# Delta-rule attention and a top-2 router in one kernel: gathered rows regrouped by transfers and turned by VectorE

## The chip, the cores and the metric

The kernel runs on one core of a Trainium2 chip. The metric is the time of one execution on the device in microseconds; lower is better. The core has five instruction queues that matter here. TensorE (PE) multiplies matrices, and its weight loads have a row of their own, PEld. VectorE (DVE), ScalarE (ACT) and GpSimd (POOL) do the elementwise work. SyncE (SP) issues transfers; GpSimd issues the indirect ones, which gather or scatter rows by a list of row numbers. Each queue runs in order, and the queues meet at semaphores.

## The reference

```python
batch, n_heads, seq, head_dim = (4, 8, 768, 48)
for t in range(S):                        # delta rule, one state per (batch, head)
    kt, vt, bt = (k_n[:, :, t], v[:, :, t], beta[:, :, t, None])
    y[:, :, t] = np.einsum('bhd,bhde->bhe', q[:, :, t], state)
    v_old = np.einsum('bhde,bhd->bhe', state, kt)
    state = state + bt[:, :, :, None] * np.einsum('bhd,bhe->bhde', kt, vt - v_old)
...
x = np.ascontiguousarray(attn_out.transpose(0, 2, 1, 3)).reshape(B * S, H * D)   # 3072 x 384
noisy_logits = x @ w_gate + np.log1p(np.exp(x @ w_noise)) * noise                # 8 experts
top2 = np.argpartition(-noisy_logits, 2, axis=1)[:, :2]
...
for e in range(E):
    for k in range(2):
        mask = top2[:, k] == e
        h = np.maximum(x[mask] @ w1[e], 0.0)          # 384 -> 1024
        out[mask] += top2_w[mask, k, None] * (h @ w2[e])   # 1024 -> 384
```

Each of 3072 tokens goes through two of eight experts. All arithmetic is in float32.

## The kernel before

**Two stages.** `deltanet` computes the recurrence in chunks of 64 tokens and, as tokens become ready, routes them. A small planner (`Jobs`) gives every piece of work an engine, a cost and a due time, and writes out the order of all engines, SP and GpSimd among them. Then the experts run one after another in an order that the code itself gives, for PE, ACT, DVE and GpSimd; SP is left to the scheduler there.

**The table of tokens.** Router results go to a table in HBM, `tokens_x`, with three floats a row: the token's number, its gate, and the row of `rows_y` where its 384 attention outputs lie. `spread` (L431) scatters them, `load_metas` (L417) and early loads (L1268) read them back as lists. Numbers are stored as floats, so `numbers` (L427, L428, and L1277, L1278 for the early tiles) has VectorE convert them to integers before an indirect transfer can use them. `take_rows` (L396) gathers rows of `rows_y` by such a list, 128 tokens to a tile; `add_rows` (L450) adds finished rows to the output.

**Expert 0** is done mostly inside the first stage. As soon as the first tiles of its tokens are known, `early` gathers them, turns them on PE (L1302), and multiplies (L1321, L1345). Five tiles are done so. What is left, one tile and 64 rows, is `rest` (L1688 to L1720): it uses `rest_x`, whose gathers stand at the end of the first stage. This place, between the stages, is called the seam. `rest` also prepares expert 1: it gathers its rows (`load_rows`), forms the sums of its first weights (`SUMS_W`, on VectorE here), turns its rows and forms the sums of them (`SUMS_X`).

**Experts 1 to 7** have six tiles of 128 tokens and one of 64 each, 832 columns. Both products use schemes with fewer multiplications on sums of blocks: `first` (the hidden layer, L1576 into `inner`, twenty block products) and `second` (L1576 into `outer` and `inner`, seven products for each of three pairs of tiles, added to `sums` by VectorE at L1475 and L1479). `both(n)` is step n for the first two pairs. While expert e runs, the rows of e + 1 are gathered into one of two buffers `xr` after `first`; `turn_rows` (L1591, L1596) turns a tile by three TensorE transpositions into a PSUM bank and a copy by ScalarE, two tiles after each of four `both` calls; then come `SUMS_X` (L1542) on VectorE and `SUMS_W` on GpSimd. A bank of PSUM can only be reused when the add that reads it is done.

Of the kernel before, what the change touches and what calls it, by code (L numbers as in the profile page):

```python
# [9 lines left out]
FP32 = mybir.dt.float32  # L10
I32 = mybir.dt.int32
# [10 lines left out]
Q = 32  # L22
TILES = 6
MORE = 64
EARLY_BANK = 2, (0, 1, 2)
EARLY = {1: [(0, 2)], 3: [(2, 4)], 4: [(4, 5)]}
EARLY_TILES = 5
ROWS = TILES * 128 + MORE
# [53 lines left out]
BANKS_C, TURN_BANKS, LAST_BANK = (1, 2, 4), (3, 0), 4  # L82
# [149 lines left out]
def kernel(  # L232
# [110 lines left out]
    w1r = moe_w1.rearrange("e (do di) f -> e di do f", di=128)  # L343
    w2r = moe_w2.rearrange("e (fo fi) d -> e fi fo d", fi=128)

    def weight_tiles(pool):
        return (
            pool.tile([128, KT, F], FP32, name="w1e"),
            pool.tile([128, FT, DM], FP32, name="w2e"),
        )  # L350

# [42 lines left out]
    def take_rows(got, index, units):  # L394
# [13 lines left out]
    indices, places = (  # L408
        const.tile([128, E, TILES + 1], I32, name=x) for x in ("indices", "places")
    )  # L410
# [15 lines left out]
    def numbers(e, t):  # L426
        nc.vector.tensor_copy(places[:, e, t], metas_x[:, e, t, 2])  # L427
        nc.vector.tensor_copy(indices[:, e, t], metas_x[:, e, t, 0])  # L428
# [31 lines left out]
    def deltanet(ictx):  # L460
# [593 lines left out]
        def route(g):  # L1054
# [91 lines left out]
            def counted():  # L1146
# [12 lines left out]
                        metas(g)[:, 0:units, :, x],  # L1159
# [54 lines left out]
        def cut(s, rows):  # L1214
# [21 lines left out]
        early_index, early_place = (  # L1236
            sb([128, EARLY_TILES], x, I32) for x in ("early_index", "early_place")
        )
        early_meta = sb([128, EARLY_TILES, META], "early_meta")

        def put_early(got, at):
            d = add_rows(got, early_index[:, at : at + 1], "out0", added)
            early_out.append(d)
            return d

        early_x = [sb([128, DM], f"early_x{i}") for i in range(4)]
# [9 lines left out]
        def early(s, lo, hi):  # L1256
# [19 lines left out]
            def numbers():  # L1276
                nc.vector.tensor_copy(early_place[:, lo:hi], early_meta[:, lo:hi, 2])  # L1277
                nc.vector.tensor_copy(early_index[:, lo:hi], early_meta[:, lo:hi, 0])  # L1278

# [3 lines left out]
            )  # L1283
            jobs.add(
                DVE, 0.4, numbers, reads=[("early_meta", lo)], writes=[("early_index", lo)],
                late=lo,
            )
            units = (s + 1) * US
            for i in range(n):
                at = lo + i  # L1290
                x, x_key = early_x[at % 4], ("early_x", at % 4)
                jobs.add(
                    POOL, 1.2,
                    lambda x=x, at=at: [take_rows(x, early_place[:, at : at + 1], units)],
                    reads=[("early_index", lo), *(("stored", i) for i in range(units))],
                    writes=[x_key], lands=2.0, moves=0.7, late=lo,
                )
                p = early_bank()

                def turned_rows(x=x, p=p):  # L1300
                    for do in range(KT):
                        nc.tensor.transpose(  # L1302
                            flat(p)[:, do * 128 : (do + 1) * 128],
                            x[:, do * 128 : (do + 1) * 128], ident,
                        )

                jobs.add(PE, 0.5, turned_rows, reads=[x_key], opens=p, late=lo)
                jobs.add(
                    ACT, 0.5,
                    lambda i=i, p=p: nc.scalar.copy(  # L1310
                        early_xe[:, :, i * 128 : (i + 1) * 128],
                        flat(p)[:, 0 : KT * 128].rearrange("p (k t) -> p k t", t=128),
                    ),
                    writes=[("early_xe", i)], closes=p, late=lo,
                )
# [21 lines left out]
            for i in range(n):  # L1337
# [3 lines left out]
                for f0 in range(0, FT, 2):  # L1341
# [19 lines left out]
                )  # L1361
                jobs.add(
                    POOL, 1.3,
                    lambda got=got, at=at: [put_early(got, at)],
                    reads=[got_key, ("early_index", lo), *(("cleared", i) for i in range(4))],
# [8 lines left out]
        held = {}  # L1374
# [14 lines left out]
        nc.gpsimd.memset(blanks[:, :, 0], float(N))  # L1389
# [48 lines left out]
        every = [("rows", x, i, y) for x in range(NS) for i in range(US) for y in (0, 1)]  # L1438
        for e in range(E):
            jobs.add(  # L1440
                SP, 0.7, lambda e=e: load_metas(e), reads=every, writes=[("metas", e)],
                lands=2.0, moves=0.3, late=EARLY_TILES - 0.5,
            )
        last_tiles = slice(EARLY_TILES, TILES + 1)
        jobs.add(
            DVE, 0.4, lambda: numbers(0, last_tiles), reads=[("metas", 0)],
            writes=["places"], late=EARLY_TILES - 0.5,
        )
        for i, size in enumerate(rows_in[last_tiles]):
            jobs.add(  # L1450
                POOL, 1.2,
                lambda i=i, size=size: take_rows(
                    rest_x[0:size, i],
                    places[0:size, 0, EARLY_TILES + i : EARLY_TILES + i + 1], NT,
                ),
                reads=["places", *(("stored", n) for n in range(NT))], writes=[("rest_x", i)],
                lands=2.0, moves=0.7, late=EARLY_TILES - 0.5,
            )
        jobs.add(
            DVE, 0.4, lambda: numbers(slice(1, E), slice(0, TILES + 1)),  # L1460
            reads=[("metas", e) for e in range(1, E)], writes=["all places"],
            late=EARLY_TILES - 0.4,
        )
# [4 lines left out]
        return held["w"]  # L1468

    with ExitStack() as ictx:  # L1470
        weights = deltanet(ictx)
# [15 lines left out]
    with ExitStack() as ectx:  # L1487
        ectx.enter_context(
            tc.manual_schedule(engines={*IN_ORDER, mybir.EngineType.Pool})
# [20 lines left out]
        xrs = [moe.tile([128, TILES + 1, DM], FP32, name=f"xr{i}") for i in range(2)]  # L1510
# [70 lines left out]
        def load_rows(e, tiles=range(TILES + 1)):  # L1581
            for i in tiles:
                take_rows(
                    xrs[e % 2][0 : rows_in[i], i], places[0 : rows_in[i], e, i : i + 1], NT
                )

        def turn_rows(e, i, banks=TURN_BANKS):
            xr, rows = xrs[e % 2], rows_in[i]
            p_xt = inner[banks[i % len(banks)]][:, 0 : KT * 128].rearrange("p (k t) -> p k t", t=128)
            for do in range(KT):  # L1590
                nc.tensor.transpose(  # L1591
                    p_xt[:, do, 0:rows], xr[0:rows, i, do * 128 : (do + 1) * 128],
                    ident[0:rows, 0:rows],
                )
            at = MAIN if rows < 128 else i * 128 + (MORE if i * 128 >= MAIN else 0)
            nc.scalar.copy(xe[:, :, at : at + rows], p_xt[:, :, 0:rows])  # L1596
# [78 lines left out]
        def rest():  # L1675
# [5 lines left out]
            got, gate = sums[0], metas_x[:, 0, :, 1]  # L1681
            load_rows(1)
            add_up(nc.vector, SUMS_W, blocks[0])
            xe_r = moe.tile([128, KT, cols], FP32, name="xe_r")
            for i, size in enumerate(rows_in[t0:]):
                p_xt = bank_x[i][:, 0 : KT * 128].rearrange("p (k t) -> p k t", t=128)
                for do in range(KT):
                    nc.tensor.transpose(  # L1688
                        p_xt[:, do, 0:size], rest_x[0:size, i, do * 128 : (do + 1) * 128],
                        ident[0:size, 0:size],  # L1690
                    )
                nc.scalar.copy(
                    xe_r[:, :, i * 128 : i * 128 + size], p_xt[:, :, 0:size]
                )
# [9 lines left out]
            for i in range(TILES + 1):  # L1704
                turn_rows(1, i, range(5))
# [7 lines left out]
            for fo in range(FT):  # L1713
# [9 lines left out]
                add_rows(got[0:size, i], indices[0:size, 0, t0 + i : t0 + i + 1], "out0", added)  # L1723
# [6 lines left out]
        index, gate = indices[:, 1], metas_x[:, 1, :, 1]  # L1730
        sums_of_second(blocks[1])
        for e in range(1, E):
# [6 lines left out]
            def put(i):  # L1739
                added.append(  # L1740
                    add_rows(
                        got[0 : rows_in[i], i], index[0 : rows_in[i], i : i + 1], f"out{e}",
                        earlier,
                    )
                )
# [23 lines left out]
            if follows:  # L1769
                load_rows(e + 1)  # L1770
                add_up(nc.gpsimd, SUMS_W, blocks[0])
# [8 lines left out]
            turns = iter(range(TILES + 1 if follows else 0))  # L1780
            sums_x = SUMS_X if follows else []
            for n in (5, 6, 3, 7, 4):
                both(n)
                for i in (next(turns, None), next(turns, None)):
                    if i is not None:
                        turn_rows(e + 1, i)
# [14 lines left out]
            if follows:  # L1801
                sums_of_second(blocks[1])
                index, gate = indices[:, e + 1], metas_x[:, e + 1, :, 1]
# [7 lines left out]
    with tc.If(count > ROWS):  # L1811
        for e in range(E):
            with tc.tile_pool(name=f"left{e}", bufs=1) as pool:
                w1e, w2e = load_weights(weight_tiles(pool), e)
                earlier, added = added, []
                for i in range(TILES, NT):
# [3 lines left out]
                    index, row = (pool.tile([128, 1], I32, name=x) for x in ("indexl", "rowl"))  # L1820
                    nc.vector.tensor_copy(index, meta[:, 0:1])
                    if i == TILES:
                        nc.vector.memset(index[0:MORE], N)
                    nc.vector.tensor_copy(row, meta[:, 2:3])
                    gate = meta[:, 1:2]
                    xr = pool.tile([128, DM], FP32, name="xrl")
                    take_rows(xr, row, NT)
# [3 lines left out]
                    for do in range(KT):  # L1831
                        nc.tensor.transpose(
                            p_xt[:, do], xr[:, do * 128 : (do + 1) * 128], ident
# [49 lines left out]
```

## Time and profile before

| | us |
|---|---|
| median of 3 runs (835.3 to 838.07) | 837.69 |
| the profiled execution | 832.74 |
| its span, from first to last instruction | 830.6 |
| `first` of expert 1 starts | 394.9 |
| one expert, from `first` to `first` | 60.6 |
| end of expert 7 on PE, about | 819 |

Times in a timeline are us from the start of the span. A row of it gives start, duration, engine, line, operation, output<-inputs, shapes, number of instructions merged, and in brackets how long the engine sat idle before and what released it. A row of the table by stage gives the stretch, its length, the busy time of PE, PEld, DVE, ACT and POOL, the granted TensorE clock as a share, the share of the DMA engines and GB/s. In the page, a digit is a fortieth of the span in tenths of busy time.

### The profile page before, as it was taken

Reading aid. Unit: us, or ns where it says so; the run is one execution under the profiler, and the core shown is the slowest. Engines: PE = TensorE matmul, PEld = TensorE weight load, DVE = VectorE, ACT = ScalarE, POOL = GpSimd, SP = SyncE. Lnnn points to the kernel's source line nnn. Section 1 sums busy time; section 2 is a strip of 40 time slices with the busy share of each in tenths; the row PEclk is TensorE's granted clock in tenths of the full one; section 3 lists DMA queues with packets and bytes.
Section 4 is the critical chain, followed back from the end, with each engine's and each line's share of the span. In section 5 each row is a group of like instructions: output and inputs, shape, how many; then the busy total and the mean of one; then the engine's idle time right before and its main releaser. Section 6 shows DMA issues by size and latency. Waiting matters only on the chain.

```text
span 830.6 us, 22834 instructions
## 1 busy us (share of the span) xinstructions
PE 734.5 (88%) x9512; PEld 577.3 (70%) x9512; DVE 550.6 (66%) x1238; ACT 332.1 (40%) x789; POOL 398.6 (48%) x377
## 2 busy tenths in 40 slices
PE   4656888786978889997999999999999999999993
PEld 3445777675767787774588588587597597597593
DVE  5899999998899343034676665665766765865841
ACT  3546585836582641122530531531521521511500
POOL 2102100134311815632885885885885786777022
PEclk9975868879798689998999999999999999999997
DMA  2465646533232311553523524425325235213022
GB/s 48 76 112 126 188 137 157 143 63 67 47 71 55 52 43 21 97 145 119 143 81 47 149 77 77 119 78 105 90 84 119 69 95 114 62 20 42 1 38 26
DMA packets 119888, 70.67 MB, mean 85 GB/s; under 512 B 93536, under 2 KB 114144, under 8 KB 119776
## 3 DMA queue, kind: packets, MB, share of 16 engines
q1 hardware_dynamic: 105056, 48.98, 22.4%
q0 software_dynamic: 12544, 19.75, 13.3%
q8 instruction: 77, 1.26, 0.7%
q10 hardware_dynamic: 2176, 0.39, 0.3%
q14 instruction: 35, 0.29, 0.1%
HBM read 49.85 MB, written 20.03 MB: 84 GB/s over the span
## 4 chain that ended last, share of the span: by engine, by line
PE 62%; DVE 20%; issue 10%; POOL 3%; DMA 2%; ACT 1%; SPq 1%; DVEq 0%; POOLq 0%; ACTq 0%
PE inner L1576 25%; PE outer L1576 14%; DVE part L737 6%; DVE t L741 5%; PE pair L1321 3%; PE pair L1345 3%; PE pair L606 2%; POOL out_dram L450 2%; PE inner L1591 2%; PE inner L1668 2%; PE single L588 2%; PE pair L924 1%; DVE t L656 1%; PE pair L983 1%; DVE qk L858 1%
## 5 line engine op out<-in xcount | busy, mean ns | idle before, releaser
L1618 DVE TENSOR_TENSOR hT<-hT,inner 128x416 f32<-128x416 f32 x182 | 105.4, 586 | 64.3 <-PE inner L1576 56.4
L450 POOL DMA_INDIRECT out_dram<-sums,indices x51 | 83.0, 1627 | 117.1 <-DVE sums L1479 68.8
L1624 ACT ACTIVATE hT<-inner 128x416 f32<-128x416 f32 x112 | 57.9, 517 | 173.0 <-PE inner L1576 172.2
L431 POOL DMA_INDIRECT tokens_x<-meta,slot x48 | 48.5, 1010 | 89.3 <-DVE r_d L1071 39.4
L1576 PE MATMUL inner<-s_x,w1e 128*128 128x416 f32 x196 | 78.7, 512 | 0.0
L737 DVE TENSOR_TENSOR part<-t 128x30 f32<-128x30 f32 (+9 forms) x180 | 70.7, 393 | 4.8
L741 DVE TENSOR_TENSOR t<-t,part 128x30 f32<-128x30 f32 (+9 forms) x180 | 63.0, 350 | 6.2
L1613 ACT ACTIVATE hT<-hT 128x416 f32<-128x416 f32 x112 | 59.8, 547 | 12.2 <-DVE hT L1618 7.2
L396 POOL DMA_INDIRECT xr<-rows_y,places x49 | 57.0, 1164 | 14.0 <-issue 13.1
L1576 PE MATMUL outer<-t_w,hT 128*128 128x192 f32 x336 | 59.7, 328 | 0.0
L1576 PEld LDWEIGHTS inner<-s_x,w1e 128*128 128x128 f32 x196 | 37.2, 190 | 31.2 <-issue 29.0
L706 POOL TENSOR_SCALAR_AFFINE_SELECT t<-t 128x1024 f32<-128x1024 f32 x6 | 7.6, 1267 | 106.5 <-DVE ss L677 106.5
L1576 PE MATMUL inner<-xe,w1e 128*128 128x416 f32 x140 | 58.1, 513 | 0.0
L1576 PE MATMUL inner<-s_x,s_w 128*128 128x416 f32 x140 | 56.9, 512 | 0.0
L1596 ACT COPY xe<-inner 128x384 f32<-128x384 f32 (+1 forms) x49 | 20.3, 459 | 90.8 <-PE inner L1591 90.8
L1576 PEld LDWEIGHTS outer<-t_w,hT 128*128 128x128 f32 x336 | 54.7, 190 | 0.4
L1576 PE MATMUL outer<-w2e,hT 128*128 128x192 f32 x280 | 50.1, 326 | 0.0
L1576 PEld LDWEIGHTS outer<-w2e,hT 128*128 128x128 f32 x280 | 46.5, 190 | 2.2 <-issue 2.2
L1542 POOL TENSOR_TENSOR w1e<-w1e 128x256 f32<-128x256 f32 x54 | 47.0, 878 | 2.0
L1475 DVE TENSOR_SCALAR sums<-outer,metas_x 128x192 f32<-128x192 f32 x70 | 28.0, 414 | 29.9 <-PE outer L1576 29.9
L888 POOL TENSOR_TENSOR v<-v,norms 128x384 f32<-128x384 f32 x24 | 22.7, 961 | 52.3 <-PE pair L606 41.9
L1576 PEld LDWEIGHTS inner<-s_x,s_w 128*128 128x128 f32 x140 | 26.6, 190 | 22.3 <-issue 22.3
(202 smaller groups left out, 1620.7 us busy)
## 6 DMA issues: line engine op xcount, KB each, us to landing
w1e<-in_moe_w_dram SPq DMA_DIRECT2D x8, 1536.0 KB
w2e<-in_moe_w_dram SPq DMA_DIRECT2D x8, 1536.0 KB
qp<-in_q_dram SPq DMA_DIRECT2D x48, 96.0 KB
v<-in_v_dram SPq DMA_DIRECT2D x48, 96.0 KB
out_dram<-empty SPq DMA_DIRECT2D x4, 1152.0 KB
rows_y<-y SPq DMA_DIRECT2D x24, 192.0 KB
kp<-in_k_dram SPq DMA_DIRECT2D x88, 48.0 KB
out_dram<-sums,indices POOLq DMA_INDIRECT x51, 4.4
```

What stands on the lines that cost most here:

```text
L396: d = nc.gpsimd.indirect_dma_start(out=got, out_offset=None, in_=rows_y[0 : units * 128], in_offset=bass.IndirectOffsetOnAxis(ap=index, ax ...
L431: d = nc.gpsimd.indirect_dma_start(out=tokens_x, out_offset=bass.IndirectOffsetOnAxis(ap=slot, axis=0), in_=meta, in_offset=None, bounds_c ...
L450: d = nc.gpsimd.indirect_dma_start(out=out, out_offset=bass.IndirectOffsetOnAxis(ap=index, axis=0), in_=got, in_offset=None, bounds_check= ...
L737: v_.tensor_tensor(out=part, in0=t[:, :, j + 1 :, j, None].to_broadcast(shape), in1=t[:, :, None, j, 0:j].to_broadcast(shape), op=ALU.mult,)
L741: columns[:] = [v_.tensor_tensor(out=t[:, :, j + 1 :, 0:j], in0=t[:, :, j + 1 :, 0:j], in1=part, op=ALU.add).ins]
L1321: nc.tensor.matmul(flat(p)[:, 0:rows], w1e[:, do, fo * 128 : (fo + 1) * 128], early_xe[:, do, 0:rows], start=(do == 0), stop=(do == KT - 1),)
L1475: nc.vector.tensor_scalar_mul(got, p, gate)
L1542: engine.tensor_tensor(out=block(to), in0=block(x), in1=block(y), op=ALU.add if sign == "+" else ALU.subtract,)
L1576: nc.tensor.matmul(p, lhsT, rhs, start=opens and i == 0, stop=i == len(products) - 1, skip_group_check=True,)
L1613: nc.scalar.activation(h, h, ACTF.Relu)
L1618: nc.vector.tensor_tensor(out=h, in0=h, in1=p, op=ALU.add if sign > 0 else ALU.subtract)
L1624: nc.scalar.mul(h, p, float(sign))
```

## The change

Five things are changed.

1. For experts 1 to 7 the gathered rows are no longer turned on TensorE. Sixteen transfers (`regroup`) move 32-row by 96-column pieces within SBUF from `xr` to a new tile `xq`, so that partition group c holds columns c*96 to c*96+95 of all tokens. Seven block transpositions of VectorE (`turns`), which turn 32x32 blocks in place of their partition group, then write `xe`. One buffer `xr` is left in place of two.
2. So that this gives a usable order, feature number di*3+do lies in partition di, chunk do (before: do*128+di). The first weights are loaded by that rule (`(di do)`), which makes 12 KB of each partition contiguous, and the blocks that TensorE still turns (early tiles, `rest_x`) are read with a step of three (`chunk`).
3. The table's numbers are integers kept in the bits of the float table; `numbers` and its tiles go.
4. At the seam, the lists, the gathers of `rest_x` and of expert 1's rows and `regroup` come first in GpSimd's order; three of the five additions of the early tiles (`held["puts"]`) come after them and after `SUMS_W`, which GpSimd does there now.
5. SP keeps the program's order in the second stage too: weights of expert 1, then the lists, `regroup`, weights of expert 2, and for each later expert its weights, then `regroup`.

```diff
-    w1r = moe_w1.rearrange("e (do di) f -> e di do f", di=128)
+    w1r = moe_w1.rearrange("e (di do) f -> e di do f", di=128)
+    def chunk(x, k):
+        return x[:, k:DM:KT]
...
-    def numbers(e, t):
-        nc.vector.tensor_copy(places[:, e, t], metas_x[:, e, t, 2])
-        nc.vector.tensor_copy(indices[:, e, t], metas_x[:, e, t, 0])
+    def number_of(meta):
+        return meta[..., 0:1].bitcast(I32)
+
+    def place_of(meta):
+        return meta[..., 2:3].bitcast(I32)
...
+                if s > PUT_IN_RULE:
+                    held["puts"].append(lambda got=got, at=at: put_early(got, at))
+                    continue
...
-        xrs = [moe.tile([128, TILES + 1, DM], FP32, name=f"xr{i}") for i in range(2)]
+        xr = moe.tile([128, TILES + 1, DM], FP32, name="xr")
+        xq = moe.tile([128, QS, TILES + 1, DM // QS], FP32, name="xq")
...
-        def turn_rows(e, i, banks=TURN_BANKS):
-            xr, rows = xrs[e % 2], rows_in[i]
-            p_xt = inner[banks[i % len(banks)]][:, 0 : KT * 128].rearrange("p (k t) -> p k t", t=128)
-            for do in range(KT):
-                nc.tensor.transpose(
-                    p_xt[:, do, 0:rows], xr[0:rows, i, do * 128 : (do + 1) * 128],
-                    ident[0:rows, 0:rows],
-                )
-            at = MAIN if rows < 128 else i * 128 + (MORE if i * 128 >= MAIN else 0)
-            nc.scalar.copy(xe[:, :, at : at + rows], p_xt[:, :, 0:rows])
+        def regroup():
+            for g in range(QS):
+                tiles = TILES + (g * Q < MORE)
+                for c in range(QS):
+                    nc.sync.dma_start(
+                        out=xq[c * Q : (c + 1) * Q, g, 0:tiles],
+                        in_=xr[
+                            g * Q : (g + 1) * Q, 0:tiles, c * DM // QS : (c + 1) * DM // QS
+                        ],
+                    )
+        def turns():
+            def turn(out, in_):
+                return lambda: nc.vector.transpose(out=out, in_=in_)
+            some = TILES // 2
+            for i in range(2):
+                for k in range(KT):
+                    yield turn(
+                        xe[:, k, full[i]].rearrange("p (i g x) -> p i g x", i=some, g=QS),
+                        xq[:, :, i * some : (i + 1) * some, k : DM // QS : KT].rearrange(
+                            "p g i j -> p i g j"
+                        ),
+                    )
+            more = MORE // Q
+            yield turn(
+                xe[:, :, MAIN : MAIN + MORE].rearrange("p k (g x) -> p k g x", g=more),
+                xq[:, 0:more, TILES].rearrange("p g (j k) -> p k g j", k=KT),
+            )
...
+            for e in range(E):
+                load_metas(e)
+            for i, size in enumerate(rows_in[t0:]):
+                take_rows(rest_x[0:size, i], place_of(metas_x[0:size, 0, t0 + i]), NT)
             load_rows(1)
-            add_up(nc.vector, SUMS_W, blocks[0])
+            regroup()
+            add_up(nc.gpsimd, SUMS_W, blocks[0])
+            for put in early_puts:
+                put()
...
-            for i in range(TILES + 1):
-                turn_rows(1, i, range(5))
+            for turn in turns():
+                turn()
             add_up(nc.vector, SUMS_X, xb)
...
                 load_rows(e + 1)
+                regroup()
                 add_up(nc.gpsimd, SUMS_W, blocks[0])
...
-            turns = iter(range(TILES + 1 if follows else 0))
+            turning = turns() if follows else iter(())
             for n in (5, 6, 3, 7, 4):
                 both(n)
-                for i in (next(turns, None), next(turns, None)):
-                    if i is not None:
-                        turn_rows(e + 1, i)
+                for turn in (next(turning, None), next(turning, None)):
+                    if turn is not None:
+                        turn()
```

A transposition by VectorE writes to SBUF, so no PSUM bank and no copy by ScalarE belong to it. The path for experts with more than 832 tokens is changed to match and isn't run with these inputs.

## Prediction

> **What bounds the kernel now.** I read the page's busy rows and its 40 slices first, then the chain of waits, then the table by stage (windows) for one expert, then the timeline of that expert and of the seam before the first of them.
>
> ```profile
> PE 734.5 (88%) x9512; PEld 577.3 (70%) x9512; DVE 550.6 (66%) x1238; ACT 332.1 (40%) x789; POOL 398.6 (48%) x377
> PE   4656888786978889997999999999999999999993
> PEclk9975868879798689998999999999999999999997
> ...
> core 0: us, PE busy (x) PEld busy (x) DVE busy (x) ACT busy (x) POOL busy (x), PEclk, DMA share, GB/s
> 377.00:385.40 8.40, 3.20 (x22) 2.27 (x20) 0.00 (x0) 2.91 (x7) 1.50 (x2) 0.76 0.69 243
> 385.40:392.20 6.80, 6.80 (x19) 3.72 (x20) 6.29 (x12) 0.32 (x1) 0.00 (x0) 0.79 0.00 0
> 516.50:577.10 60.60, 60.60 (x286) 45.63 (x285) 39.36 (x69) 19.29 (x39) 45.07 (x40) 1.00 0.37 93
> ```
>
> From slice 15 on TensorE is at nine tenths or more with a full clock, and one expert (516.5 to 577.1) is 60.6 us of TensorE with no hole. So in this half each us taken from PE's queue is a us of the run, if nothing else becomes late. VectorE has 21 us free there. The one hole is the seam, 377 to 385.4: PE 3.2 us busy of 8.4, its clock at 0.76 and 0.79 after it.
>
> **Part 1: the transpositions leave PE** (six experts, 2 to 7; those of expert 1 are in part 3). In the chain of waits an expert is 27.93 us of `first`, 168 matmul records of `second` at 0.1625 us (2.60 for 16) = 27.3, and 2.73 of `last_rows`; 2.7 of 60.65 is left. The timeline shows it:
>
> ```profile
> 491.20 0.74 PEld L1591 LDWEIGHTS inner<-ident,xr 128*128 128x128 f32 x6
> 491.91 2.58 PEld L1576 LDWEIGHTS outer<-t_w,s_h 128*128 128x128 f32 x16
> ...
> 501.23 0.26 PEld L1591 LDWEIGHTS inner<-ident,xr 64*128 64x128 f32 x3 [0.23 <-issue]
> 501.55 2.57 PEld L1576 LDWEIGHTS outer<-t_w,hT 128*128 128x128 f32 x16
> 502.07 1.59 DVE L1542 TENSOR_TENSOR s_x<-xe 128x416 f32<-128x416 f32 x3 [0.31 <-ACT xe L1596]
> ```
>
> Six transpositions hold the weight queue from 491.20 to 491.91, 0.71 us, three times; the last three cost 0.32 and the 0.23 of idle before them. That is 2.68 us an expert, 16.1 in six. ScalarE's seven copies (19.3 of 60.6 busy) were beside the path and give nothing.
>
> A page speaks against the move: the Trainium skill, "VectorE: DVE Perf Modes", section "Rules for kernel authors", wants a 128x128 transposition on TensorE wherever PSUM will do, as this kernel had it. Its table's 390 ns, in 21 pieces, would make 8.2 us of PE (an estimate from the page); the trace has 2.7. By either, PE is the engine with no hole and VectorE the one with 21 us, so I keep the trace's 2.7.
>
> **Part 2: what VectorE takes on.** Per expert six block transpositions (turns, from here) of 128x384 and one of 128x192. The nearest rows:
>
> ```profile
> L656 DVE STREAM_TRANSPOSE t<-gd 128x1024 f32<-128x1024 f32 x6 | 11.6, 1934 | 0.4 <-ACT gd L639 0.4
> L720 DVE STREAM_TRANSPOSE norms<-norm 128x32 f32<-128x32 f32 x6 | 1.1, 186 | 0.0
> ```
>
> The line through both is 1.76 ns an element: 0.81 us for 384, 0.47 for 192. Back-to-back VectorE instructions overlap by 0.09 (1.22 us at 52.58, the next at 53.71), so 0.72 and 0.38: 4.7 us an expert, VectorE 44 of 58 us. The end that matters is order. VectorE runs in program order, and PE reuses a bank only after VectorE's add from it. A round of PE is now 2.60 us; VectorE has two adds (0.73) and two turns (1.44) in it, 2.17, so it keeps up. After the last turn come five sums of `SUMS_X` (2.7 us) and only then the adds of step 4, at about 502.8 on the old clock of the expert; step 1 of the third pair, which reopens outer0 at 503.06, waits for the first of them: 0.2 us. Net gain 2.46 an expert, **14.8** in six. Bounds: at 0.5 a turn 2.6 an expert; at 1.0 (if GpSimd's sums beside it stretch a turn as they do L1564, 0.95 alone and up to 1.48) step 4 waits 0.9 us and 1.7 is left; at 1.2, 0.4.
>
> **Part 3: `regroup`, a new wait.** Sixteen transfers on SP, which VectorE's first turn waits for. They start when the last gather lands: 474.59 plus 3.1 (median to landing of xr's gathers) = 477.7. SP issues 128 pieces in 0.32 to 0.38 us (rows_y) and 512 in 0.64 (qp, v), so about 0.42 for 192 to 224 pieces, 6.7 for sixteen. A small load lands 1.6 us after its issue starts (early_meta at 328.85, first used 330.47). So the rows are there 8.5 us later, at 486.2; at 28 ns a packet (queue q1: 22.4% of 16 engines' 830.6 us over 105,056 packets) 3,328 packets on 16 engines are 5.9, which is under the issue time. The first turn has its place behind the adds of step 5, about 492 to 492.9: 6 us of slack, so I cost it at nothing. Cover ends when `regroup` takes more than 15.2 us from the last landing; then each us is a us of PE, since the adds queue behind the turn and the banks behind them. On SP the next w1e stands behind it (483.1 becomes about 485) and isn't read before 536. GpSimd's order per expert is unchanged.
>
> Here too a page warns: the Trainium skill, "SBUF — State Buffer", section "The DMA setup-cost knee", has some 2 us fixed per transfer and asks for one large one. One after another, sixteen would take 32 us by that (an estimate): 17 us of stall an expert. The trace's row for small ones in a queue:
>
> ```profile
> 340.62 6.53 SPq L417 DMA_DIRECT2D metas_x<-tokens_x  x8
> 349.85 0.19 DVE L427 CAST places<-metas_x 128x49 int32<-128x49 f32 x1 [6.02 <-DMA metas_x<-tokens_x]
> ```
>
> Eight, of up to 896 pieces, are issued in 6.53 us and all have landed 2.7 us after that: the fixed part is paid once, not eight times. I take the row.
>
> **Part 4: the seam.**
>
> ```profile
> 367.67 1.55 POOL L450 DMA_INDIRECT out_dram<-early_x,early_index  x1 [10.12 <-DVE most L1515]
> 369.52 1.32 POOL L396 DMA_INDIRECT xr<-rows_y,places  x1 [0.30 <-issue]
> 382.40 0.87 PE L1591 MATMUL inner<-ident,xr 128*128 128x128 f32 x3 [3.48 <-DMA xr<-rows_y,places]
> 384.89 0.55 PE L1591 MATMUL inner<-ident,xr 64*128 64x64 f32 x3 [1.62 <-DMA xr<-rows_y,places]
> 385.37 6.83 PE L1709 MATMUL outer<-w2e,hT 128*128 128x384 f32 x16
> ```
>
> Expert 1's gathers stand on GpSimd behind an addition that waits for PE's last early tile, and run into the w1e load of 377. In the new order they follow rest_x's gathers (which end at 347.8): 348.2 to 357.5 (9.3 us for seven, as now), landed 359.7. On SP the loads of expert 1's weights now come before the lists (the metas_x loads), not after: their tiles were last read near 307, so they start at about 329.2 behind early_meta, not 347.26, take the 10 us that they take now, and are gone before the lists and gathers. `regroup` to 368.2, turns to 372.9, the twelve sums of `SUMS_X` (6.4 us, 385.83 to 392.19) to 379.3. `SUMS_W`, now GpSimd's: 21 at 0.727 = 15.3 us, 357.5 to 373. The three held additions (5.7 us) follow and only feed the output. PE: its part of `rest` ends at 376.96, then L1709 follows with no hole: at full clock 16 of that shape take 5.25 (L1345: 32 in 10.5), not 6.83, and L1714 2.73, so `first` starts at 384.95 instead of 394.87: **9.9** gained, with 5.6 us to spare on VectorE and 11 on GpSimd. If the lists or gathers land 6 us later, nothing is lost; beyond that, us for us.
>
> **Part 5: the rest.** The conversions leave VectorE and the early gathers move up in GpSimd's order (in front of v at 229.5, about 225 to 228). They share the stage's latency chain: between 1.5 lost and 1.5 gained; I take 0. PE now reads 21 blocks (15 early, 6 of rest_x) with a step of three elements; no row shows a weight load with a step: nothing, or twice the 0.14 us, 2.9 in all; near the row, 0.5 lost.
>
> **Sum.** 14.8 + 9.9 - 0.5 = 24.2. The profiled execution took 832.74 us (span 830.6, 2.1 around it): 808.5. The median of the runs, 837.69, is 4.95 above it; the change takes nothing from that difference, so 813.5.
>
> **Rivals.** (a) The forecast, 813.5, its own range 809 to 817: 0.62; 0.07 more for a stage of the recurrence that comes out faster, 808. (b) VectorE becomes the bound of an expert's second half: turns of 1.0 to 1.2 us leave 2 to 10 of the 14.8, so 818 to 826: 0.12. For it L1564's spread; against it, a turn has one input. (c) The seam stays, because lists, gathers or `regroup` collide there with the weight loads (as at 382.4): 823: 0.07. (d) **Slower**: `regroup` is late in every expert. Each us over 15.2 counts six times, over 14.1 once in the seam: with 24.2 to lose it breaks even at 18.5 us, 1.15 us a transfer; at 20 it is 848, one after another 932. For it: four v loads took 6.21 us at 105 with 1152 KB transfers in the queue; against it, DMA share is 0.00 from 478 to 484. 0.09. (e) Both gains eaten, within 0.3% (2.5 us, about what a measurement can tell from none): 0.03.
>
> Faster 0.88, same 0.03, slower 0.09. The range 808 to 826 takes in (a), (b), (c).
>
> **What would show it.** Period of an expert 58.2 us with PE at 100%; a turn near 0.81; the last xq transfer landed before the turn's place, with no PE wait for VectorE over 0.3; the w1e of expert 1 issued near 329 and `first` starting near 385 with a clock of 1.00 before it. Wrong would be: xq transfers spaced by a us or more, or a first turn that waits for DMA.

## The result, and the profile after

| | before | after |
|---|---|---|
| median of 4 runs, us | 837.70 (835.30 to 838.07) | 816.79 (814.37 to 819.58) |
| the profiled execution / its span | 832.74 / 830.6 | 819.58 / 817.8 |
| `first` of expert 1 starts | 394.87 | 395.50 |
| one expert, from `first` to `first` | 60.65 | 58.47 |

The ratio is 0.9757, with a 95% interval of 0.9720 to 0.9795: 20.9 us faster by the medians. The two profiled executions differ by only 13.2 us, because the one of before was faster than each of its four runs and the one of after is the slowest of its own. So the two profiles cannot simply be subtracted: stretches have to be compared that start and end at the same piece of work.

The page of the kernel after, its first rows (busy time of each engine; then PE's busy tenths and its granted clock in 40 slices):

```profile
PE 727.6 (89%) x9365; PEld 572.8 (70%) x9365; DVE 566.7 (69%) x1256; ACT 311.6 (38%) x740; POOL 414.3 (51%) x398
PE   4665887887889889999999999999999999999993
PEclk9955789768868656999999999999999999999998
```

TensorE has 147 products fewer (the 49 times three transpositions), VectorE 16 us more. Slices 15 and 16 of the clock row, counted from one, read 5 and 6, where before had 8 and 9: the first stage ran differently, and that is not the experts' doing.

**The experts.** The table by stage of one expert after (the columns are those of the table before), and TensorE's timeline in its second half:

```profile
512.50:571.00 58.50, 58.46 (x266) 43.53 (x265) 42.97 (x76) 16.39 (x32) 45.23 (x40) 1.00 0.48 119
```

```profile
545.67 2.76 PE L1548 MATMUL inner<-t_w,s_h 128*128 128x192 f32 x16
548.27 2.76 PE L1548 MATMUL outer<-t_w,s_h 128*128 128x192 f32 x16
550.87 2.76 PE L1548 MATMUL inner<-w2e,s_h 128*128 128x192 f32 x16
553.47 5.36 PE L1548 MATMUL outer<-t_w,hT 128*128 128x192 f32 x32
558.67 1.46 PE L1548 MATMUL outer<-t_w,s_h 128*128 128x192 f32 x8
560.18 1.57 PE L1548 MATMUL outer<-w2e,hT 128*128 128x192 f32 x8
```

Before, three groups of six transpositions and one of three stood between these rounds:

```profile
549.42 2.76 PE L1576 MATMUL inner<-t_w,s_h 128*128 128x192 f32 x16
552.02 0.82 PE L1591 MATMUL inner<-ident,xr 128*128 128x128 f32 x6
...
564.91 1.46 PE L1576 MATMUL outer<-t_w,s_h 128*128 128x192 f32 x8
```

The rounds of 16 products now follow each other at 2.60 us with nothing between. From the first of them to the first product of the third pair it was 549.42 to 564.91 before, 15.49 us, and is 13.00 now: 2.49 us are gone. Of these 0.31 are lost again just behind. The last row of the kernel after starts 1.51 us after the one above it, where eight products need 1.30, and `last_rows` 1.50 after that, where before had 1.40. The weight queue says for what TensorE waits, and VectorE's timeline says why:

```profile
560.18 1.27 PEld L1548 LDWEIGHTS outer<-w2e,hT 128*128 128x128 f32 x8 [0.34 <-DVE sums L1444]
```

```profile
548.85 1.30 DVE L1572 STREAM_TRANSPOSE xe<-xq 128x384 f32<-128x384 f32 x2
550.06 0.39 DVE L1444 TENSOR_SCALAR sums<-outer,metas_x 128x192 f32<-128x192 f32 x1
...
556.61 0.43 DVE L1572 STREAM_TRANSPOSE xe<-xq 128x192 f32<-128x192 f32 x1
557.07 1.59 DVE L1514 TENSOR_TENSOR s_x<-xe 128x416 f32<-128x416 f32 x3
558.70 0.59 DVE L1514 TENSOR_TENSOR xe<-xe 128x416 f32<-128x416 f32 x1
559.21 0.58 DVE L1514 TENSOR_TENSOR s_x<-xe,s_x 128x416 f32<-128x416 f32 x1
559.71 0.74 DVE L1444 TENSOR_SCALAR sums<-outer,metas_x 128x192 f32<-128x192 f32 x2
```

Two turns take 1.30 us, and the next instruction starts 1.21 us after the first of them: a turn is about 0.65 us, and 0.61 from start to start. The five sums stand between the last turn and the adds of step 4, which end at 560.4.

**The seam.** Two rows of TensorE before, then SyncE's queue, TensorE's and VectorE's timeline of the kernel after:

```profile
361.41 5.33 PE L1345 MATMUL pair<-w2e,early_hT 128*128 128x384 f32 x16
374.85 2.11 PE L1699 MATMUL inner<-xe_r,w1e 128*128 128x192 f32 x12
```

```profile
333.87 0.38 SPq L359 DMA_DIRECT2D w1e<-in_moe_w_dram  x1
...
369.23 10.47 SPq L1562 DMA_DIRECT2D xq<-xr  x16
```

```profile
371.99 5.33 PE L1337 MATMUL pair<-w2e,early_hT 128*128 128x384 f32 x16
...
385.56 2.11 PE L1697 MATMUL inner<-xe_r,w1e 128*128 128x192 f32 x12
387.51 5.32 PE L1707 MATMUL outer<-w2e,hT 128*128 128x384 f32 x16
392.77 2.80 PE L1712 MATMUL outer<-w2e,hT 128*64 128x384 f32 x16
395.50 1.66 PE L1548 MATMUL inner<-xe,w1e 128*128 128x416 f32 x4
```

```profile
381.25 3.98 DVE L1572 STREAM_TRANSPOSE xe<-xq 128x384 f32<-128x384 f32 x7 [2.82 <-DMA xq<-xr]
```

The products of `rest` run into each other at full clock, and the expert follows without a hole. From the start of the last early tile's second product (16 products of 128x384, at 361.41 before and 371.99 after) to the start of `first` it was 33.46 us and is 23.51: 9.95 gained. Of this, 8.57 are the transpositions with their two waits, and 1.51 the full clock of the product after them; 0.13 goes the other way. But that product itself starts 10.58 us later than before, and so all of the seam's gain is gone in this pair of profiles. This lateness is the open question. VectorE waits at 381.25 for `regroup`, 12.0 us after its first transfer was issued.

### The profile page after: what moved, and what is told of

Read it like the earlier page. It is cut to its first block, busy times and chain, and to the rows that moved or that the text cites. A ratio compares the mean times of both kernels' runs of the same rounds, so it can differ in the third digit from the quotient of the medians.

```text
span 817.8 us, 22648 instructions
## 1 busy us (share of the span) xinstructions
PE 727.6 (89%) x9365; PEld 572.8 (70%) x9365; DVE 566.7 (69%) x1256; ACT 311.6 (38%) x740; POOL 414.3 (51%) x398
## 4 chain that ended last, share of the span: by engine, by line
PE 60%; DVE 21%; issue 10%; POOL 3%; SPq 2%; ACT 1%; DMA 0%; DVEq 0%; POOLq 0%; ACTq 0%
PE inner L1548 25%; PE outer L1548 14%; DVE part L743 6%; DVE t L747 5%; PE pair L1313 3%; PE pair L1337 3%; PE pair L612 2%; POOL out_dram L456 2%; PE inner L1659 2%; PE single L1004 1%; SPq L546 1%; DVE t L662 1%; DVE qk L864 1%; PE pair L989 1%; SPq L562 1%
## 5 line engine op out<-in xcount | busy, mean ns | idle before, releaser
L456 POOL DMA_INDIRECT out_dram<-sums,metas_x x51 | 83.6, 1639 | 94.4 <-DVE sums L1448 67.1
L401 POOL DMA_INDIRECT xr<-rows_y,metas_x x49 | 56.4, 1152 | 14.0 <-issue 13.0
L1548 PE MATMUL outer<-t_w,hT 128*128 128x192 f32 x336 | 58.0, 326 | 0.0
L1514 POOL TENSOR_TENSOR w1e<-w1e 128x256 f32<-128x256 f32 x63 | 53.5, 858 | 2.3
L1548 PEld LDWEIGHTS inner<-xe,w1e 128*128 128x128 f32 x140 | 26.4, 190 | 20.7 <-issue 16.2
L801 ACT COPY w<-tt 32x256 f32<-32x256 f32 x96 | 38.6, 402 | 5.5 <-DVE tt L778 3.5
```

Of the source, the lines that this page charges most:

```text
L401: d = nc.gpsimd.indirect_dma_start(out=got, out_offset=None, in_=rows_y[0 : units * 128], in_offset=bass.IndirectOffsetOnAxis(ap=index, ax ...
L456: d = nc.gpsimd.indirect_dma_start(out=out, out_offset=bass.IndirectOffsetOnAxis(ap=index, axis=0), in_=got, in_offset=None, bounds_check= ...
L801: lambda rows=rows, cols=cols, w64=w64, tt=tt: nc.scalar.copy(w64[rows, :, cols], tt[rows]),
L1514: engine.tensor_tensor(out=block(to), in0=block(x), in1=block(y), op=ALU.add if sign == "+" else ALU.subtract,)
L1548: nc.tensor.matmul(p, lhsT, rhs, start=opens and i == 0, stop=i == len(products) - 1, skip_group_check=True,)
```

## The experiments

All eight runs came from one chip, on which the kernel before took 858.27 us (median of 11) in the first four and 856.28 (of 9) in the others. Times are compared within this group only. Stretches that run at full clock are comparable everywhere. This table holds what is read from each profile: when the last early tile's second product starts (the end of the first stage, in effect), the seam from there to `first`, and the period of experts 2 to 6.

| run | first stage ends | seam | period |
|---|---|---|---|
| before, first profile | 361.4 | 33.46 | 60.65 |
| after, first profile | 372.0 | 23.51 | 58.47 |
| before again | 395.9 | 34.26 | 60.65 |
| after again | 385.3 | 23.51 | 58.47 |
| copies back | 389.4 | 23.51 | 58.47 |
| sums later | 383.2 | 25.19 | 59.35 |
| experts on TensorE | 380.1 | 23.51 | 60.90 |
| transfers twice | 381.2 | 25.51 | 66.2 to 67.5 |
| turns twice | 376.1 | 23.52 | 61.05 to 62.3 |
| additions first | 377.1 | 38.00 | 58.47 |

**Both kernels again.** No edit.

> The changed kernel once more, unchanged, for a second profile of the first stage. In the first profiles the last early tile's second product on TensorE (32 products of 128x384) started at 344.5 us before and at 355.1 after, 10.6 us later, and from 295 to 321 us the granted clock was 0.50 after against 1.00 from 300 us on before. Theory A (luck of the clock): this profile has that product elsewhere, between 345 and 352, and the times scatter over 814 to 820 with a median near 817. Theory B (the new order of the first stage makes the clock fall there each time): again 353 to 357 with 0.50 from 295 to 320.

> The kernel before once more, for a second profile of it. The seam is taken from the start of the last early tile's second product (16 products of 128x384) to the start of first: 33.46 us before in the first profile, 23.51 in three profiles of the changed one. Theory A: the seam's 9.95 us are the order's, and this profile has 33 to 34 again, whatever the first stage took. Theory B: they hung on that one run's transfers and clock, and it has 26 to 31. Expert's period 60.65 by both.

Measured: the kernel after 831.98 us (829.47 to 834.23, 6 runs), ratio to before 0.9694 (0.9660 to 0.9728). The kernel before had one more execution for its profile, 868.15, which is 12 us above its median there. Period and seam come back to the hundredth for the kernel after; for the kernel before the period does, and the seam is 34.26, a little over what was put, with L1709 at 8.00 us in place of 6.83. So theory A of the seam holds. The end of the first stage moved by 13 us for the kernel after and by 34 for the kernel before, with the granted clock: for the kernel before it was 0.97 and 0.66 in the first two stretches of 50 us in the first profile, and 0.65 and 0.57 here. Neither expectation for the first stage holds as it was put: the clock from 295 on doesn't repeat (0.50 until 310 here, full from 315), but the product named there starts at 368.35, neither between 345 and 352 nor between 353 and 357, and the median isn't near 817, because the whole group is slower. What the pair of first profiles showed, the first stage 10.6 us later after, is turned round here: 10.6 us earlier. Both differences rest on one profile of each kernel, and the one of before was a long execution here. Over all ten profiles the first stage ends later where its mean granted clock, up to that end, is lower: 361.4 at 0.83 and 372.0 at 0.78 in the first pair, 385.3 at 0.75 and 395.9 at 0.73 here (correlation -0.92). What sets that clock from one execution to the next stays open.

**The order of the first stage put back.** The early tiles' row numbers are copied by VectorE again, so that all engines have the order of before in the first stage.

```diff
+            def numbers():
+                nc.vector.tensor_copy(early_place[:, lo:hi, None], place_of(early_meta[:, lo:hi]))
+                nc.vector.tensor_copy(early_index[:, lo:hi, None], number_of(early_meta[:, lo:hi]))
+            jobs.add(DVE, 0.4, numbers, reads=[("early_meta", lo)], writes=[("early_index", lo)], late=lo)
```

> VectorE copies the early tiles' row numbers to tiles of their own again (integers to integers), so that the planner gives the first stage exactly the order of before on every engine; experts and seam stay as changed. The parts that could be read from the two profiles are 13.1 us gained in six experts and 9.9 at the seam, 23.0, and the medians differ by 20.9, so 2.1 us are missing. Theory A (the missing 2 us are the new order of the first stage): 2 to 3 us faster than the changed kernel, near 814.5. Theory B (they are scatter of the first stage, or the weights' own loading): within 1 us of the changed kernel, near 817.

Measured: 836.25 us (832.98 to 837.18, 6 runs), 4.3 slower than the kernel after; ratio to before 0.9738 (0.9705 to 0.9772), whose interval overlaps that of the kernel after. Theory A fails in its sign. Theory B's bound of 1 us is missed too. With the first stage in the order of before, the rest of the change gains 22.0 us by the medians; what the profiles give for experts and seam is 13.1 and 9.95, 23.1. That fits. Whether the new order of the first stage is itself worth something is not settled: 2 us lost in the first runs (20.9 against 23.1), 3 to 4 gained on this chip, and the end of the first stage scatters by 9 us over the six kernels here that keep its new order or all but the place of three additions (376.1 to 385.3, one profile each).

**The experts turned by TensorE again.** Only experts 2 to 7; expert 1 keeps transfers and turns. `turn_rows` is that of before, three transpositions and a copy by ScalarE, but reads `chunk(xr, do)`.

```diff
                 load_rows(e + 1)
-                regroup()
...
-                    if turn is not None:
-                        turn()
+                    if turn is not None:
+                        turn_rows(turn)
```

> Experts 2 to 7 are turned by TensorE and copied by ScalarE again, without the sixteen transfers; the seam (expert 1) keeps transfers and VectorE's turns, and the first stage and the layout stay as changed. Theory A (the turns' leaving TensorE is worth 2.18 us an expert): period 60.65, run 13.1 us slower than the changed kernel, near 830. Theory B (part of the period's gain comes from elsewhere, such as SP's order or the quieter ScalarE): period under 60, run 5 to 10 us slower, 822 to 827.

Measured: 842.22 us (839.75 to 844.78, 4 runs), 10.2 slower than the kernel after, period 60.90. The periods account for 6 x 2.43 = 14.6; the first stage ended 5 us earlier in this run's profile. Theory A holds: all of the period's gain goes with the turns, and 0.25 us beyond it. The groups of the weight queue show where these come from. Two lines of those groups, of this kernel and of the kernel before, each over one expert (count, busy us, mean ns of one, idle before):

```profile
L1573 PEld LDWEIGHTS inner<-ident,xr 128*128 128x128 f32 x18 | 2.4, 197 | 0.0
```

```profile
L1591 PEld LDWEIGHTS inner<-ident,xr 128*128 128x128 f32 x18 | 2.2, 141 | 0.1
```

Here the transposed block is read with a step of three elements, before it was contiguous: 197 ns for 141. That is the cost of a strided weight load that no row of before showed, and on the path 21 of them cost the 0.25 us. The fifteen early blocks, read with the same step in the kernel after, show it too: 203 ns, and 147 before.

**Each turn twice.**

```diff
-                return lambda: nc.vector.transpose(out=out, in_=in_)
+                return lambda: [nc.vector.transpose(out=out, in_=in_) for _ in range(2)]
```

> Each block transposition is done twice, for the price of a turn. Theory A (VectorE has 2 us left in the three rounds of turns, and the adds queue behind): 4.3 us more of VectorE make TensorE 2.8 to 3.1 us later in each expert, period 61.2 to 61.6, longer than before's 60.65, run up by 17 to 19 us. Theory B (VectorE has its free time where the turns are, as its 23 free us an expert suggest): period 58.5 to 59.3, run up by less than 5 us.

Measured: 844.57 us (840.78 and 848.36, 2 runs), 12.6 above the kernel after; period 61.05 to 61.07 in four experts, 61.42 and 62.3 in the others. Theory A holds, its size a little less than put: the six periods add 17.0 us, and the first stage of this profile ended 9 us earlier. TensorE's timeline:

```profile
563.03 2.76 PE L1548 MATMUL outer<-t_w,hT 128*128 128x192 f32 x16
568.18 2.84 PE L1548 MATMUL outer<-t_w,hT 128*128 128x192 f32 x16 [2.39 <-DVE sums L1448]
```

TensorE waits here, for an add that stands behind four turns. 4.3 us more on VectorE became 2.6 us on TensorE, although VectorE is idle for 15 us of an expert: its idle time lies elsewhere. At twice its price the turn would have eaten the whole gain of the experts.

**The sixteen transfers twice.**

```diff
-            for g in range(QS):
+            for g in (*range(QS), *range(QS)):
```

> The sixteen transfers are issued twice, one set after the other, for the price of their lateness. Now they are issued in 10.4 us from 476.8 and the first turn stands at 490.4, 13.6 us after their start. Theory A (issue sets their time, 0.65 us each): landed 22 to 23 us after their start, VectorE waits 8.8 us for them at the first turn, the expert's period rises by about 8 us to 66.5, the seam by 6.5, the run by about 54 us. Theory B (transfers of the two sets overlap on the DMA engines): landed within 16 us, period below 61, run up by less than 15 us.

Measured: 888.96 us (888.89 and 889.03, 2 runs), 57 above the kernel after. SyncE's queue, VectorE and TensorE in one expert:

```profile
504.21 20.79 SPq L1562 DMA_DIRECT2D xq<-xr  x32
```

```profile
526.77 1.26 DVE L1572 STREAM_TRANSPOSE xe<-xq 128x384 f32<-128x384 f32 x2 [9.00 <-DMA xq<-xr]
```

```profile
519.75 2.76 PE L1548 MATMUL inner<-w2e,s_h 128*128 128x192 f32 x16
528.47 1.94 PE L1548 MATMUL outer<-t_w,hT 128*128 128x192 f32 x5 [5.96 <-DVE sums L1444]
```

Theory A holds in an expert: 32 transfers are issued at 0.65 us each, the rows are there 22.6 us after the first, VectorE stands still for 9 us, and the adds behind the turn hold TensorE's banks. Only at the seam it was put otherwise than it came: 2.0 us there instead of 6.5, but 16 in expert 1 behind it (74.7 us), twice what the others lose. This is the mechanism of the forecast's slower rival, at a lateness that the real kernel doesn't have. Set beside the kernel after, where the first turn of an expert starts 13.6 us after the first transfer and isn't made to wait, and where the seam shows 12.0 us from issue to last landing, it says that some 1.6 us of slack are left (an estimate; in the kernel after, the last packet of `regroup` ends 11.5 us after the first issue at 476.8, and 11.6 after it at the seam).

**The additions of the early tiles first again.**

```diff
-PUT_IN_RULE = 1
+PUT_IN_RULE = 9
```

> The three additions of the early tiles stand ahead of the gathers of rest_x and of expert 1's rows on GpSimd again; all else stays as changed. Theory A (their place ahead of the gathers is what made the seam): the gathers wait for the last early product, expert 1's rows are regrouped 25 us later, the seam grows from 23.5 to between 40 and 44, run up by 16 to 20 us. Theory B (the early weights and the sums on GpSimd made it): seam 24 to 28.

Measured: 849.74 us (846.78 to 857.45, 8 runs), 17.8 above the kernel after. GpSimd, TensorE, and the table by stage of TensorE alone (its columns: stretch, length, PE busy, granted clock, DMA share, GB/s):

```profile
383.34 1.55 POOL L456 DMA_INDIRECT out_dram<-early_x,early_meta  x1 [10.13 <-DVE most L1487]
385.19 1.08 POOL L401 DMA_INDIRECT rest_x<-rows_y,metas_x  x1 [0.30 <-issue]
```

```profile
415.08 3.11 PE L1548 MATMUL inner<-xe,w1e 128*128 128x416 f32 x4 [5.29 <-issue]
421.52 1.72 PE L1548 MATMUL inner<-s_x,s_w 128*128 128x416 f32 x2 [3.33 <-DVE s_x L1514]
```

```profile
409.70:415.00 5.30, 0.09 (x2) 0.91 0.88 305
415.00:428.00 13.00, 9.60 (x14) 0.51 0.49 144
428.00:440.00 12.00, 12.00 (x36) 1.00 0.24 66
```

The addition that waits 10 us for the last early tile holds all gathers behind it, and `regroup` starts at 399.1 instead of 369.2, which is 24.8 us later counted from the end of the first stage. The seam grows by 14.5 us, less than put, but expert 1 takes 66.6 us in place of 58.6, so that 22.5 are lost in all (16 to 20 were expected). The other 8 are a wait for the sums of the rows and a clock of 0.51 for 13 us after the hole. So the seam's gain needs the three additions behind the gathers: early weights, and sums on GpSimd, which this kernel keeps, are no use without it. The other way round was not tried: the new order alone, with late weights or with TensorE's transpositions kept at the seam.

**The sums of the rows later.** A try at the 0.31 us, and a miss.

```diff
-                if n == 7:
+                if n == 4:
                     add_up(nc.vector, sums_x[0:5], xb)
```

> The first five sums of the rows are placed behind step 4 of the first two pairs instead of ahead of it, so that VectorE's adds of step 4 no longer queue behind 2.7 us of sums. Theory A (TensorE loses 0.3 us an expert to these adds, as the profile shows at 560.18): the expert's period falls from 58.47 to 58.16 to 58.2 and the run by 1.6 to 1.9 us in six experts. Theory B (the adds were waiting for TensorE anyway, or the later sums delay the adds of the third pair as much): period 58.4 to 58.6, run unchanged within 0.5 us.

Measured: 836.07 us (832.53 to 840.37, 6 runs), period 59.35. Theory B, and worse than it put: 0.88 us an expert lost.

```profile
574.61 1.46 PE L1548 MATMUL outer<-w2e,hT 128*128 128x192 f32 x8
...
580.18 1.46 PE L1548 MATMUL outer<-w2e,s_h 128*128 128x192 f32 x8
582.53 1.57 PE L1548 MATMUL outer<-t_w,hT 128*128 128x192 f32 x8 [0.89 <-DVE sums L1444]
```

```profile
390.81 6.82 PE L1697 MATMUL inner<-xe_r,w1e 128*128 128x192 f32 x30 [0.41 <-ACT xe_r L1690]
```

The wait at step 4 is indeed gone (the first row starts 1.30 after its predecessor at 573.31), but the sums now stand ahead of the third pair's adds, and TensorE waits there, longer. The seam of 25.19, which this edit doesn't touch, is a matter of the clock: TensorE did the same work in the same order, but 30 of its products took 6.82 us, where the kernel after needed 5.14, with the granted clock at 0.79 from 390 to 398. Placing one of the five sums later, not all, was not tried. Nor was it tried whether a second issuing queue would bring the rows sooner. No kernel of this study beats the changed one.

## Why the prediction was right

The forecast was 813.5 us, its own range 809 to 817, the whole range 808 to 826; the median is 816.79. It was the forecast's case, near the upper end of its own range, and of its 24.2 us 20.9 came. The 3.3 that are missing: 1.7 in the experts, nothing at the seam, and 1.6 that the medians leave over for the first stage.

- **Part 1, mis-sized.** 2.68 us an expert were put down for the transpositions, 2.49 were removed. The 0.71 us were read from the start of the six weight loads to the start of the next group; but that group was followed by its own successor after 2.55 us instead of 2.60, so that a set of six was worth 0.65. The Trainium skill's rule of a 128x128 transposition on TensorE ("VectorE: DVE Perf Modes", "Rules for kernel authors") would have kept 2.5 us of TensorE an expert in place of 4.3 of VectorE and sixteen transfers, which is the smaller amount of work. That TensorE had no free time and VectorE had decided it, as was argued.
- **Part 2, right in its mechanism.** A turn took 0.61 us from start to start (forecast 0.72), and the wait came from the adds of step 4 behind the five sums of `SUMS_X`, as put: 0.31 us for 0.2. The group that waits is step 1 of the third pair, as put. Together 2.18 an expert, 13.1 in six, for 14.8. Doubled turns, some 1.3 us each, left nothing: 0.40 us an expert more than before. The bounds given, 1.7 left at 1.0 us and 0.4 at 1.2, run on to 0.25 lost at 1.3 (an estimate), so they were about right. Rival (b) feared that GpSimd's sums stretch a turn as they do L1564. They do stretch L1564, which has two inputs: 0.95 us with no such sum beside it, 1.11 to 1.48 with one. A turn of 128x384 took 0.65 to 0.68 us without and 0.66 to 0.72 with one in the kernel after, so this fear had no ground.
- **Part 3, right, with less to spare than thought.** Issue was 0.65 us a transfer, not 0.42: the estimate from the number of pieces in transfers to and from HBM was too low. It took the shortest issues of `rows_y`, 0.32 to 0.38 us, while their median in the kernel before is 0.55. The rows took 12.0 us, not 8.5, and the 6 us of slack were about 1.6: 3.5 went with the rows, and about 1 because the first turn comes 13.6 us after the first transfer, not 14.5. That nothing was lost here is thus in part luck. The Trainium skill's fixed 2 us ("SBUF — State Buffer", "The DMA setup-cost knee"), read as one transfer after another, would have had 32 (an estimate): the trace's row for the lists was nearer, at 0.82 us each. The slower rival had the right mechanism; the doubled transfers gave 57 us.
- **Part 4, right.** 9.9 forecast, 9.95 measured, and 10.75 in a second pair (34.26 to 23.51). Its pieces: the holes, the transpositions, and the clock of L1709. That the weights' issue came at 333.9 and not 329, and `first` at 395.5 and not 385, is the first stage's lateness alone. `regroup` took its 12 us here too, and VectorE's time to spare covered it: 5.6 us were forecast, and 3.9 were left (its sums end at 391.6, `first` starts at 395.5).
- **Part 5, the step that was too sure.** The strided reads cost 0.25 us for 21 blocks, in the experiment with TensorE's turns, as little as was put (0.5). But the first stage was given a bound of 1.5 us to either side, and its end moves by 9 us between profiles of one order, more than the change can be shown to move it. The medians leave 2.1 us lost there for the change in the first runs, and 3.2 gained (26.3 us in all) in the later ones. That the 24.2 lie between is luck as far as this stage goes.

## What to carry to other kernels

Where one engine has no hole, moving work off it pays at the price that work has *between* its neighbours in that queue; what it costs on the other engine is read from the order in which that engine's results are waited for, not from its idle share (4.3 us more on an engine with 15 us idle cost 2.6 us here). At a seam, look in each queue for the instruction that waits longest and only feeds the output, and put it behind what the next stage needs. When a stage ahead of the change scatters by a good part of what the change is worth (9 us of 21 to 26 here), measure the change over stretches between the same two pieces of work, and keep that stage's scatter in the range.

## What the hardware showed beside

- **A hole can cost twice.** After TensorE had been idle for 5.3 us, its granted clock was 0.51 for the next 13 us, with another hole of 3.3 us in them, and four products of 128x416 took 3.11 us instead of 1.66; with the transfers doubled it was 0.74 in the stretch after a hole of 6 us. This agrees with the Trainium skill, "TensorE: Matmul & The Clock Gate", section "Why this matters for your kernels", which asks for no idle gaps over some 3 us between bursts. Shorter holes mostly didn't do it: with the turns doubled, five of six holes of 2.4 to 2.65 us were followed by a clock of 1.00 and one by 0.73, which made the expert of 62.3 us. Nor does every low clock follow a hole: in "sums later" it fell at the seam with no idle time over 0.66 us ahead of it. The part of the seam's gain that was clock (1.51 us) stood behind two holes, of 3.48 and 1.62 us.
- **A step of three elements (12 bytes) in a weight load isn't free**: 197 ns for 141.
- **GpSimd's sums slow some work of VectorE and not other**: up to 1.48 us for 0.95 in an addition or subtraction of two tiles, at most 0.72 for 0.68 in a turn.
- **Sixteen small transfers within SBUF** in one queue need 0.65 us each to issue, and so do 32; the rows were used 1.6 to 1.8 us after the end of the last issue.
